# One batch turn of an attention and maxout kernel put in another order: scores inside the first layer, state read beside S.W

## The chip, the cores and the metric

The kernel runs on one core of a Trainium2 chip. A core has a matrix engine (TensorE, PE in the profile, with its weight loads as PEld), three engines for elementwise work (VectorE = DVE, ScalarE = ACT, GpSimd = POOL) and a queue engine (SyncE = SP) that here issues all transfers of the loop. TensorE writes only into eight PSUM banks, and the other engines copy results from there. Engines run side by side, each in its own order, and wait for each other by semaphores. The metric is the device time of one execution, in microseconds.

## The reference, cut to what matters

```python
# x: 8 batches, 8 heads, 512 tokens, 64 wide; state: 8, 8, 32 slots, 64
scale = 1.0 / np.sqrt(D)
scores = scale * np.matmul(x, state.transpose(0, 1, 3, 2))      # 512 x 32
a = softmax(scores)                                             # over the slots
xread = np.matmul(a, state)
scores2 = scale * np.matmul(state, x.transpose(0, 1, 3, 2))     # 32 x 512
sread = np.matmul(softmax(scores2), x)                          # over the tokens
tokens = concatenate([xread, sread], axis=2)    # 8 x 544 tokens of 512 (heads side by side)
return np.maximum(tokens @ w1, tokens @ w2) @ w_out             # w1, w2: 512 x 1024; w_out: 1024 x 512
```

## The kernel before, in words

`max(t w1, t w2) = t w2 + relu(t (w1 - w2))`, so the kernel forms `wd = w1 - w2` and `wwo = w2 w_out` once. The read of a token is linear in the softmax A, so per batch it forms S.W (`sw_mm`: the state's block-diagonal form `sbd` times `wd` and `wwo`) and never writes `xread`. What is done for a batch b:

- x in two casts to bf16: `cast_e` (for the state read, tile `xe`) and `cast_b` (tile `xb`), the latter transposed by a DMA (`xt_dma`, x^T in `xt`);
- `sc_mm`, `sc_ev`: scores from x^T in two halves, 8 matmuls each, exp on ScalarE into `e`; `red` sums and inverts on VectorE, `mul` scales to A (tile `a`) on GpSimd, and `at_dma` transposes A by a DMA into `at`;
- `sr_mm`: the state read, 32 matmuls of `e` with `xe` in TensorE tiles of 128 x 32; `sr_ev` scales it by the sums, `sr_tr` and `sr_cp` transpose it into `sread_t`;
- `sw_mm`: 24 matmuls in tiles of 64 x 32 into six half-used banks, evicted by `sw_ev`;
- the first layer: `l1_mm`, 8 pieces f of two 512-column matmuls, relu by `l1_ev` into `r`;
- the second layer as seven `product`s of 8 matmuls of 256 columns instead of eight (sums of halves of r are formed by `r_sum` on VectorE, partial results parked by `keep` and added by `put`), with four `opened` of 4 matmuls that add A^T times S.W's part for `wwo`;
- `store` writes the 1 MB of results.

The table `ORDER` writes out by hand the order of the weights' work and of batches 0 and 1. The loop at the end of the program runs `b` from 2 to 6, one turn each: first and second layer of batch b, together with scores, A, S.W and state read of batch n = b+1, loads of b+4, casts of b+2 and b+3, and a share of the tokens that come from the state. Batch 7 and those tokens follow behind the loop. The order of the calls is the order on each engine; nothing reschedules it. PSUM banks are dealt out by a ring of five ("r") and three fixed ones (`BX`, `BY`, `BZ`) for the products pX, pY, pZ. All transfers of the loop stand in one SP queue in the order of the calls; an issue waits on SP until its semaphores allow it, and what is behind it waits too.

Of the kernel before, what the change touches and what calls it, by code (L numbers as in the profile page):

```python
# [38 lines left out]
rs.0.0>V rs.0.1>V re.1.3>A p2o.1 ldx.3.0 ldx.3.1 ldx.4.0 ldx.4.1 p1.0@1 k0.0>A p1.1@4 rs.0.2>V wt.2>V v00.0 p6.0  # L39
rs.0.3>V k0.1>A k1.0>A p5.0@7 wt.3>V v00.1 rs.1.0>V k2.0>A sc.2.0@6 exp.2.0>A sc.2.1@0 exp.2.1>A sw.2.0@5,3 red.2.0>V  # L40
mul.2.0>P red.2.1>V swe.2.0.0>A swe.2.0.1>A ce.2.0>A ce.2.1>A ce.2.2>A ce.2.3>A p7.0 o7.0 v11.0 rs.1.1>V mul.2.1>P
p3.0 o3.0 rs.1.2>V atd.2 sw.2.w@6,2 swe.2.w.0>A v01.0 swe.2.w.1>A p4.0 o4.0 rs.1.3>V ce.3.0>P cb.3.0>P cb.3.1>P xtd.3
ce.3.1>P ce.3.2>P ce.3.3>P v10.0>A store.0 dif.1>P sr.2@0 p6.1 k1.1>A sw.2.1@5,3 sre.2>V swe.2.1.0>A swe.2.1.1>V
p5.1@7 k2.1>A p7.1 o7.1 v11.1 p3.1 o3.1 v01.1 srt.2@0 srte.2>A p4.1 o4.1 v10.1>A ldx.5.0 ldx.5.1
"""
# [9 lines left out]
def kernel(  # L55
# [9 lines left out]
    nc = tc.nc  # L65
    B, H, S, D = x.shape
# [38 lines left out]
    def many(n, name, shape, dtype=BF16):  # L105
        return [sbuf.tile([128, *shape], dtype, name=f"{name}{i}") for i in range(n)]
# [127 lines left out]
    def cast_b(b, g, eng):  # L234
        copy(eng, xb_s[b % 2][:, :, 256 * g:256 * g + 256].rearrange("p c (i d) -> p i c d", i=4),
             xf(b)[:, 4 * g:4 * g + 4, :].rearrange("p i (c d) -> p i c d", c=NC))

    def xt_dma(b):
        nc.sync.dma_start_transpose(out=xt_s[b % 2].rearrange("p c k t -> p (c k) t"),
                                    in_=xb_s[b % 2].rearrange("p c m -> p (c m)"))  # L240
# [14 lines left out]
    def sc_mm(b, hh, ring="r"):  # L255
        p = bank(ring)
        pv = p.rearrange("p (c g i n) -> p c i g n", c=NC, g=2, i=2)
        for c in range(NC):
            for kk in range(2):
                k = 2 * hh + kk  # L260
                nc.tensor.matmul(pv[:, c, kk], xt_s[b % 2][:, c, k, :], sbd[:, b, k, :],  # L261
                                 start=(c == 0 and kk == 0), stop=(c == NC - 1 and kk == 1))
        return p
# [110 lines left out]
    def l1_mm(b, f, ring="r"):  # L374
        p = bank(ring)
        for g in range(2):
            nc.tensor.matmul(p, sw_s[b % 3][:, g, f * 128:(f + 1) * 128], at_s[b % 3][:, g].rearrange("p c t -> p (c t)"),  # L377
                             start=(g == 0), stop=(g == 1))
# [46 lines left out]
    def product(pv, lhs, rhs, first=False, cc=(0, 1)):  # L425
        for c in cc:
            for f in range(4):
                nc.tensor.matmul(pv[c], lhs[:, f, 128 * c:128 * c + 128], rhs[:, f, :],  # L428
                                 start=first and f == 0 and (c == 0 or pv.split), stop=False, skip_group_check=True)
# [35 lines left out]
    def so_half(b, k):  # L465
        return sw_s[b % 3][:, :, FF + 256 * k:FF + 256 * k + 256]
# [266 lines left out]
    difference(2, "P")  # L733
    for g in range(2):
        cast_b(4, g, "P")
    for b in range(2, B - 1):
        n = b + 1
        if b + 2 < B and b != 3:
            xt_dma(b + 2)
        if b < 4:  # L740
            nc.vector.reciprocal(rr_all[:, b - 2], srd[:, b - 2, 0:130:129])
        for f in range(NF):
            l1_ev(l1_mm(b, f), b, f)
        pX, pY, pZ = Pair(BX), Pair(BY), Pair(BZ)
        pp = [sc_mm(n, hh) for hh in range(2)]
        for hh in range(2):
            sc_ev(pp[hh], n, hh)
        product(pX, rq(b, 0, 0), wq(0, 0), True)
        keep(0, pX, "A")
        r_sum(b, 0, "V")  # L750
        red(n, 0)
        mul(n, 0, "P")
        r_sum(b, 1, "V")
        product(pZ, rq(b, 0, 1), wq(1, 0), True)
        opened(b, pZ, 0, so_half(b, 0))
        pg = [sw_mm(n, 512 * z, 512 * z + 512, BY if z == 0 else "r") for z in range(3)]
        sw_ev(pg[0], n, 0, 512, 0, "A")
        sw_ev(pg[0], n, 0, 512, 1, "A")
        red(n, 1)
        mul(n, 1, "P")  # L760
        at_dma(n)
        if b == 3:
            xt_dma(b + 2)
        if b == 2:
            store(1)
        if b + 4 < B - 1:
            for g in range(2):
                load_x(b + 4, g)
        elif b + 4 < B:
            load_x(b + 4, 0, n=H)  # L770
        r_sum(b, 2, "V")
        product(pX, st[:, 1], wt[:, 1])
        sw_ev(pg[1], n, 512, 1024, 0, "A")
        keep(1, pX, "A")
        put(b, 0, 0, pZ, 0)
        sw_ev(pg[1], n, 512, 1024, 1, "V")
        sw_ev(pg[2], n, 1024, 1536, 0, "A")
        product(pY, st[:, 0], wt[:, 0], True)
        keep(2, pY, "A")
        r_sum(b, 3, "V")  # L780
        sw_ev(pg[2], n, 1024, 1536, 1, "A")
        if b + 2 < B:
            for k in range(4):
                cast_e(b + 2, k, "P")
        difference(n, "P")
        if b + 3 < B:
            for g in range(2):
                cast_b(b + 3, g, "P")
        if b < 6:
            v_sum(b - 2, "P")  # L790
        product(pX, st[:, 2], wt[:, 2])
        opened(b, pX, 1, so_half(b, 1))
# [114 lines left out]
```

## Time and profile before

| | us |
|---|---|
| median of 3 runs (143.96 to 144.49) | 143.96 |
| span of the profiled execution, first to last instruction | 141.9 |
| TensorE busy | 132.1 |
| VectorE busy | 103.9 |
| ScalarE busy | 88.4 |
| GpSimd busy | 72.6 |

Of the profiled execution the page gives its span and no other time. Busy times overlap: a matmul's record runs on until its results stand in the bank, while the next one has already started. For TensorE the differences of starts are therefore read. A row of the timeline has start, length, engine, line, operation, tiles and count. Lines are those of the kernel before; a helper's line (L404 for every addition, L99 for every ScalarE copy) stands for all of its calls. In the changed kernel a line is inserted at L123, so that L404 there is L405, while L99 stays L99.

### The profile page before, as it was taken

How to read it: one execution, taken by the hardware profiler on the slowest of the kernel's cores; microseconds unless marked ns; L12 is line 12 of the kernel's file. 1: busy time of each engine (PE TensorE's matmuls, PEld its weight loads, DVE VectorE, ACT ScalarE, POOL GpSimd, SP SyncE). 2: the span in 40 equal slices, each digit the busy share in tenths (PEclk: the TensorE clock that was granted, in tenths of full speed). 3: DMA queues.
4: the chain of work that ended last, by engine and by line, in shares of the span. 5: the costliest groups of instructions: out<-in, count | busy, mean ns of one | idle time of the engine just before them, and what ended most of it. 6: DMA issues, size and time to landing. Idle time of an engine off the chain costs nothing.

```text
span 141.9 us, 3651 instructions
## 1 busy us (share of the span) xinstructions
PE 132.1 (93%) x1432; PEld 93.6 (66%) x1442; DVE 103.9 (73%) x193; ACT 88.4 (62%) x172; POOL 72.6 (51%) x99
## 2 busy tenths in 40 slices
PE   6585999999999999999999999999999999999980
PEld 2264735456787776786778577857876786788860
DVE  3488969778999748984898489569948986848320
ACT  4367968886599547665874769087737745753220
POOL 4147326089109993599179809963980544200000
PEclk9999999999999999999999999999999999999998
DMA  4999999954999999999947999669217041502073
GB/s 120 332 372 389 388 381 388 347 100 78 180 316 288 72 273 259 248 255 270 390 167 137 222 385 161 134 222 225 48 34 296 2 79 69 229 0 79 2 257 120
DMA packets 36452, 29.50 MB, mean 208 GB/s; under 512 B 22608, under 2 KB 32336, under 8 KB 35536
## 3 DMA queue, kind: packets, MB, share of 16 engines
q1 hardware_dynamic: 36160, 29.10, 74.9%
q8 instruction: 12, 0.20, 0.6%
q10 hardware_dynamic: 272, 0.13, 0.3%
q14 instruction: 8, 0.07, 0.1%
HBM read 15.20 MB, written 8.91 MB: 170 GB/s over the span
## 4 chain that ended last, share of the span: by engine, by line
PE 85%; DMA 6%; DVE 2%; SPq 2%; ACT 1%; issue 1%; DVEq 0%
PE bank L428 36%; PE bank L377 18%; PE bank L434 10%; DMA big<-in_moe_w_dram 6%; PE bank L354 5%; PE bank L608 5%; PE bank L475 2%; PE bank L517 2%; PE bank L261 2%; PE bank L301 2%; SPq L164 1%; PE bank L515 1%; DVE w2m L101 1%; DVE r L372 1%; PE bank L550 1%
## 5 line engine op out<-in xcount | busy, mean ns | idle before, releaser
L372 DVE TENSOR_SCALAR r<-bank 128x512 bf16<-128x512 f32 x32 | 21.9, 690 | 13.0 <-PE bank L377 11.9
L277 POOL TENSOR_TENSOR a<-e,er 128x512 bf16<-128x512 bf16 x14 | 17.2, 1235 | 27.4 <-ACT big L99 16.3
L99 ACT COPY big<-bank 128x512 f32<-128x512 f32 (+2 forms) x40 | 21.9, 552 | 12.8 <-PE bank L434 5.5
L377 PE MATMUL bank<-at,sw 128*128 128x512 bf16 x120 | 29.1, 379 | 0.6 <-DVE sw L101 0.2
L428 PEld LDWEIGHTS <-big 128*128 128x128 bf16 x256 | 23.9, 98 | 6.1 <-DVE big L404 2.1
L99 ACT CAST sw<-bank 128x512 bf16<-128x512 f32 x36 | 20.1, 609 | 6.0 <-PE bank L354 6.0
L428 PE MATMUL bank<-big,big 128*128 128x256 bf16 x192 | 23.1, 273 | 0.1
L404 DVE TENSOR_TENSOR big<-bank,big 128x512 f32<-128x512 f32 (+1 forms) x25 | 16.5, 663 | 8.3 <-PE bank L434 7.9
L377 PEld LDWEIGHTS <-sw 128*128 128x128 bf16 x128 | 12.2, 97 | 13.5 <-ACT sw L99 0.5
L370 ACT ACTIVATE r<-bank 128x512 bf16<-128x512 f32 x32 | 18.3, 596 | 4.1 <-PE bank L377 3.9
L428 PEld LDWEIGHTS <-r 128*128 128x128 bf16 x192 | 18.2, 98 | 2.7 <-issue 0.5
L103 POOL CAST xe<-big 128x512 bf16<-128x512 f32 x23 | 15.6, 709 | 6.2 <-DMA big<-in_x_dram 6.2
L103 POOL CAST xb<-big 128x1024 bf16<-128x1024 f32 x12 | 13.1, 1111 | 4.7 <-DMA big<-in_x_dram 4.7
L428 PE MATMUL bank<-wo,r 128*128 128x256 bf16 x128 | 15.5, 273 | 0.0
L434 PE MATMUL bank<-sw,at 128*128 128x256 bf16 x96 | 14.4, 273 | 0.0
L99 ACT COPY sread_t<-bank 128x128 bf16<-128x128 bf16 x8 | 3.2, 472 | 17.3 <-PE bank L338 14.0
L434 PEld LDWEIGHTS <-at 128*128 128x128 bf16 x128 | 12.5, 98 | 1.7
L404 DVE TENSOR_TENSOR big<-r 128x1024 bf16<-128x1024 bf16 x16 | 11.6, 723 | 0.6
L273 DVE TENSOR_REDUCE sums<-e 128x16 f32<-128x512 bf16 x16 | 10.8, 674 | 0.0
L269 ACT ACTIVATE e<-bank 128x512 bf16<-128x512 f32 x16 | 8.9, 596 | 1.9 <-PE bank L261 1.4
L404 POOL TENSOR_TENSOR big<-sw 128x512 bf16<-128x512 bf16 x8 | 9.2, 1150 | 1.3 <-issue 1.3
L101 DVE CAST sw<-bank 128x512 bf16<-128x512 f32 x12 | 7.9, 681 | 1.0 <-PE bank L354 1.0
(100 smaller groups left out, 181.8 us busy)
## 6 DMA issues: line engine op xcount, KB each, us to landing
big<-in_x_dram SPq DMA_DIRECT2D x14, 512.0 KB, 7.8
out_dram<-big SPq DMA_DIRECT2D x7, 1024.0 KB, 6.0
big<-in_moe_w_dram SPq DMA_DIRECT2D x8, 512.0 KB, 11.5
big<-in_moe_w_out_dram SPq DMA_DIRECT2D x4, 512.0 KB, 11.0
big<-in_x_dram SPq DMA_DIRECT2D x1, 1024.0 KB, 6.9
out_dram<-big SPq DMA_DIRECT2D x4, 256.0 KB, 2.7
sf<-in_state_dram SPq DMA_DIRECT2D x1, 384.0 KB, 10.4
out_dram<-w2m SPq DMA_DIRECT2D x2, 128.0 KB, 2.4
```

Source lines behind the costliest of these rows:

```text
L99: nc.scalar.copy(o, i)
L101: nc.vector.tensor_copy(o, i)
L103: nc.gpsimd.tensor_copy(o, i)
L269: nc.scalar.activation(out=e_view(e_s[b % 2], hh).rearrange("p (g c) i n -> p g c (i n)", g=2), in_=p.rearrange("p (c g m) -> p g c m", c= ...
L273: nc.vector.tensor_reduce(es_all[:, b, hh], e_view(e_s[b % 2], hh), axis=AXX, op=ALU.add)
L277: (nc.gpsimd if eng == "P" else nc.vector).tensor_mul(e_view(a_s[b % 2], hh), e_view(e_s[b % 2], hh), er_s[b % 2][:, hh].unsqueeze(3).to_b ...
L370: nc.scalar.activation(out=o, in_=p, func=ACTF.Relu)
L372: nc.vector.tensor_scalar(o, p, scalar1=0.0, scalar2=None, op0=ALU.max)
L377: nc.tensor.matmul(p, sw_s[b % 3][:, g, f * 128:(f + 1) * 128], at_s[b % 3][:, g].rearrange("p c t -> p (c t)"), start=(g == 0), stop=(g = ...
L404: (nc.gpsimd if eng == "P" else nc.vector).tensor_tensor(o, i0, i1, op=op)
L428: nc.tensor.matmul(pv[c], lhs[:, f, 128 * c:128 * c + 128], rhs[:, f, :], start=first and f == 0 and (c == 0 or pv.split), stop=False, ski ...
L434: nc.tensor.matmul(pv[c], at_s[b % 3][:, g, 2 * i + c, :], rhs[:, g, :], start=False, stop=False, skip_group_check=True)
```

## The change

The turn is written in another order:

- `sc_mm` of batch b+1 stands inside the first layer (first half behind piece 1, second half behind piece 3), in banks BZ and BY in place of the ring; `red` and `mul` follow behind pieces 1 and 5, and `at_dma` is issued right behind the layer. The layer's eight evictions go to ScalarE and VectorE by the letters AVAVAAAV in place of in turn.
- The state read moves from behind the fifth product to behind the first, right in front of S.W, in bank BZ. ScalarE copies its 130 columns into `raw`, a piece of SBUF; `sr_ev` later reads that.
- The second product and its opening move from in front of S.W to behind it.
- `xt_dma(b+3)` is issued right behind `cast_b(b+3)`, in the turn in which the cast is made, in place of the head of the next turn (in b = 3: behind that turn's `at_dma`). GpSimd does these casts ahead of `difference`.
- In `ORDER`, `cast_b` and the transposition of batch 3 go ahead of its first `cast_e`.
- The flag that chooses the general path (a matmul and a copy) moves from the end of turn 6 to behind the first layer of batch 7.

```diff
-p3.0 o3.0 rs.1.2>V atd.2 sw.2.w@6,2 swe.2.w.0>A v01.0 swe.2.w.1>A p4.0 o4.0 rs.1.3>V ce.3.0>P cb.3.0>P cb.3.1>P xtd.3
+p3.0 o3.0 rs.1.2>V atd.2 sw.2.w@6,2 swe.2.w.0>A v01.0 swe.2.w.1>A p4.0 o4.0 rs.1.3>V cb.3.0>P cb.3.1>P xtd.3 ce.3.0>P
...
+    raw = rs_o[:, 0, 0:130]
...
+    xt_dma(4)
     for b in range(2, B - 1):
         n = b + 1
-        if b + 2 < B and b != 3:
-            xt_dma(b + 2)
...
         for f in range(NF):
-            l1_ev(l1_mm(b, f), b, f)
-        pX, pY, pZ = Pair(BX), Pair(BY), Pair(BZ)
-        pp = [sc_mm(n, hh) for hh in range(2)]
-        for hh in range(2):
-            sc_ev(pp[hh], n, hh)
-        product(pX, rq(b, 0, 0), wq(0, 0), True)
-        keep(0, pX, "A")
-        r_sum(b, 0, "V")
-        red(n, 0)
-        mul(n, 0, "P")
-        r_sum(b, 1, "V")
-        product(pZ, rq(b, 0, 1), wq(1, 0), True)
-        opened(b, pZ, 0, so_half(b, 0))
-        pg = [sw_mm(n, 512 * z, 512 * z + 512, BY if z == 0 else "r") for z in range(3)]
...
-        red(n, 1)
-        mul(n, 1, "P")
+            l1_ev(l1_mm(b, f), b, f, "AVAVAAAV"[f])
+            if f in (1, 3):
+                sc_ev(sc_mm(n, f // 2, (BZ, BY)[f // 2]), n, f // 2)
+            if f in (1, 5):
+                red(n, f // 4)
+                mul(n, f // 4, "P")
         at_dma(n)
-        if b == 3:
-            xt_dma(b + 2)
...
+        pX, pY, pZ = Pair(BX), Pair(BY), Pair(BZ)
+        product(pX, rq(b, 0, 0), wq(0, 0), True)
+        r_sum(b, 0, "V")
+        r_sum(b, 1, "V")
+        keep(0, pX, "A")
+        copy("A", raw, sr_mm(n, BZ)[:, 0:130])
+        pg = [sw_mm(n, 512 * z, 512 * z + 512, BY if z == 0 else "r") for z in range(3)]
+        sw_ev(pg[0], n, 0, 512, 0, "A")
+        sw_ev(pg[0], n, 0, 512, 1, "A")
+        product(pZ, rq(b, 0, 1), wq(1, 0), True)
+        opened(b, pZ, 0, so_half(b, 0))
...
-        difference(n, "P")
         if b + 3 < B:
             for g in range(2):
                 cast_b(b + 3, g, "P")
+            xt_dma(b + 3)
+        difference(n, "P")
...
-        p = sr_mm(n, "r")
-        put(b, 1, 1, pX, 2)
-        sr_ev(p, n)
+        sr_ev(raw, n)
...
+        put(b, 1, 1, pX, 2)
```

On TensorE the state read (L301 before, L302 now) and S.W (L354, L355) come together. Here is the entry into S.W of turn b=2, before, with the opening of the second product (L434) ahead of it:

```order
L434 LDWEIGHTS at2_101
L434 MATMUL bank0_63<-sw2_104,at2_101 128x256
L354 LDWEIGHTS sbd0_74
L354 MATMUL bank7_70<-wd0_75,sbd0_74 32x512
L354 LDWEIGHTS sbd0_74
```

And now, the same place, with the end of the state read ahead of it:

```order
L302 LDWEIGHTS e1_92
L302 MATMUL bank0_63<-xe0_84,e1_92 32x65
L355 LDWEIGHTS sbd0_74
L355 MATMUL bank7_70<-wd0_75,sbd0_74 32x512
L355 LDWEIGHTS sbd0_74
```

S.W used to follow 256-column matmuls on the whole array; it now follows the state read's small tiles.

SP's queue from the x^T of batch 4 (xt0) on, before; `at` rows are A^T, `out` rows are stores, `in_x` rows loads:

```order
L239 DMA_TRANSPOSE xt0_87<-xb0_89 128x16x128
L282 DMA_TRANSPOSE at0_99<-a1_94 128x8x128
L470 DMA out_0_dram<-big2_111 128x2048
L164 DMA big8_117<-in_x_dram 128x4x256 x2
L470 DMA out_0_dram<-big7_116 128x2048
L282 DMA_TRANSPOSE at1_100<-a0_93 128x8x128
L239 DMA_TRANSPOSE xt1_88<-xb1_90 128x16x128
L164 DMA big0_109<-in_x_dram 128x8x256
```

And now:

```order
L240 DMA_TRANSPOSE xt0_87<-xb0_89 128x16x128
L283 DMA_TRANSPOSE at0_99<-a1_94 128x8x128
L471 DMA out_0_dram<-big2_111 128x2048
L165 DMA big8_117<-in_x_dram 128x4x256 x2
L240 DMA_TRANSPOSE xt1_88<-xb1_90 128x16x128
L471 DMA out_0_dram<-big7_116 128x2048
L283 DMA_TRANSPOSE at1_100<-a0_93 128x8x128
L165 DMA big0_109<-in_x_dram 128x8x256
```

The x^T of batch 5 (xt1) moved up past batch 4's A^T (at1) and past store 2 (big7).

On ScalarE, the part of turn b=2 from the last scores' exp or relu to the last S.W cast, before (big6 is where `keep` parks, sw0 is S.W of batch 3):

```order
L269 ACTIVATE e1_92<-bank3_66 128x8x64
L99 COPY big6_115<-bank4_67 128x512
L99 CAST sw0_102<-bank7_70 128x512
L99 CAST sw0_102<-bank1_64 128x512
L99 CAST sw0_102<-bank6_69 128x512
L99 COPY big6_115<-bank4_67 128x512
L99 CAST sw0_102<-bank5_68 128x512
L99 COPY big6_115<-bank7_70 128x512
L99 CAST sw0_102<-bank3_66 128x512
```

And now:

```order
L371 ACTIVATE r0_105<-bank6_69 128x512
L99 COPY big6_115<-bank4_67 128x512
L99 COPY w2m0_80<-bank0_63 128x130
L99 CAST sw0_102<-bank7_70 128x512
L99 CAST sw0_102<-bank5_68 128x512
L99 CAST sw0_102<-bank3_66 128x512
L99 CAST sw0_102<-bank6_69 128x512
L99 COPY big6_115<-bank4_67 128x512
L99 CAST sw0_102<-bank2_65 128x512
```

A copy of 130 columns (w2m, the tile that `raw` is a part of) stands behind the first parked product, and one S.W cast more ahead of the second.

More of the change, by code (lines that the diff above doesn't have):

```diff
@@ L742 @@
         for f in range(NF):
-            l1_ev(l1_mm(b, f), b, f)
-        pX, pY, pZ = Pair(BX), Pair(BY), Pair(BZ)
-        pp = [sc_mm(n, hh) for hh in range(2)]
-        for hh in range(2):
-            sc_ev(pp[hh], n, hh)
-        product(pX, rq(b, 0, 0), wq(0, 0), True)
-        keep(0, pX, "A")
-        r_sum(b, 0, "V")
-        red(n, 0)
-        mul(n, 0, "P")
-        r_sum(b, 1, "V")
-        product(pZ, rq(b, 0, 1), wq(1, 0), True)
-        opened(b, pZ, 0, so_half(b, 0))
-        pg = [sw_mm(n, 512 * z, 512 * z + 512, BY if z == 0 else "r") for z in range(3)]
-        sw_ev(pg[0], n, 0, 512, 0, "A")
-        sw_ev(pg[0], n, 0, 512, 1, "A")
-        red(n, 1)
-        mul(n, 1, "P")
+            l1_ev(l1_mm(b, f), b, f, "AVAVAAAV"[f])
[4 more added lines that the diff above has]
+                mul(n, f // 4, "P")
         at_dma(n)
-        if b == 3:
-            xt_dma(b + 2)
         if b == 2:
@@ L770 @@
             load_x(b + 4, 0, n=H)
+        pX, pY, pZ = Pair(BX), Pair(BY), Pair(BZ)
[9 more added lines that the diff above has]
+        opened(b, pZ, 0, so_half(b, 0))
         r_sum(b, 2, "V")
+        sw_ev(pg[1], n, 512, 1024, 0, "A")
         product(pX, st[:, 1], wt[:, 1])
-        sw_ev(pg[1], n, 512, 1024, 0, "A")
+        sw_ev(pg[1], n, 512, 1024, 1, "V")
+        put(b, 0, 0, pZ, 0)
+        sw_ev(pg[2], n, 1024, 1536, 0, "A")
         keep(1, pX, "A")
-        put(b, 0, 0, pZ, 0)
-        sw_ev(pg[1], n, 512, 1024, 1, "V")
-        sw_ev(pg[2], n, 1024, 1536, 0, "A")
         product(pY, st[:, 0], wt[:, 0], True)
+        sw_ev(pg[2], n, 1024, 1536, 1, "A")
         keep(2, pY, "A")
         r_sum(b, 3, "V")
-        sw_ev(pg[2], n, 1024, 1536, 1, "A")
         if b + 2 < B:
@@ L792 @@
         opened(b, pX, 1, so_half(b, 1))
-        p = sr_mm(n, "r")
-        put(b, 1, 1, pX, 2)
-        sr_ev(p, n)
+        sr_ev(raw, n)
         if b < 4:
             srd_ev(b - 2)
+        put(b, 1, 1, pX, 2)
+        product(pY, st[:, 3], wq(1, 1))
+        opened(b, pY, 0, so_half(b, 1))
         if n == B - 1:
             check_sums()
-        product(pY, st[:, 3], wq(1, 1))
-        opened(b, pY, 0, so_half(b, 1))
         put(b, 0, 1, pY, 1)
@@ L811 @@
                 m_sum(k, aq, sst, "P")
-            p = bank("r")
-            nc.tensor.matmul(p[:, 0:1], full, bad, start=True, stop=True)
-            nc.vector.tensor_copy(flag[0:1, :], p[0:1, 0:1])
         store(b)
@@ L820 @@
         l1_ev(l1_mm(b, f), b, f)
-    for k in (0, 1, 2, 3):
+    p = bank("r")
+    nc.tensor.matmul(p[:, 0:1], full, bad, start=True, stop=True)
+    r_sum(b, 0, "V")
+    nc.vector.tensor_copy(flag[0:1, :], p[0:1, 0:1])
+    for k in (1, 2, 3):
         r_sum(b, k, "V")
```

## The prediction

> **What bounds the kernel now.** I read the head of the page first, then its chain, then busy times turn by turn, then one turn on TensorE in order of time.
>
> ```profile
> span 141.9 us, 3651 instructions
> PE 132.1 (93%) x1432; PEld 93.6 (66%) x1442; DVE 103.9 (73%) x193; ACT 88.4 (62%) x172; POOL 72.6 (51%) x99
> PE 85%; DMA 6%; DVE 2%; SPq 2%; ACT 1%; issue 1%; DVEq 0%
> ...
> 65.33:78.61 13.28, 13.23 (x164) 9.57 (x163) 10.18 (x19) 8.99 (x19) 9.39 (x11) 1.00 0.78 228
> ```
>
> The last row is turn b=3 of the loop (window, its length, then busy time of PE, PEld, DVE, ACT, POOL, the granted clock, the DMA share, GB/s). TensorE is busy 13.23 of 13.28 us at granted clock 1.00, and 85% of the chain is its own. No engine makes it wait by much, so earlier scores, an earlier A and an earlier x^T have no large wait to remove. A gain must come out of TensorE's own row of work, and a loss comes from anything that now arrives late. Here is turn b=3 on TensorE (start, length, line):
>
> ```profile
> 65.33 3.62 PE L377 MATMUL bank<-at,sw 128*128 128x512 bf16 x15
> 68.79 0.63 PE L261 MATMUL bank<-sbd,xt 128*128 128x64 bf16 x16
> 69.25 1.91 PE L428 MATMUL bank<-wo,r 128*128 128x256 bf16 x16
> 71.00 0.60 PE L434 MATMUL bank<-sw,at 128*128 128x256 bf16 x4
> 71.53 0.63 PE L354 MATMUL bank<-wd,sbd 64*32 64x512 bf16 x16
> 71.97 0.40 PE L354 MATMUL bank<-wwo,sbd 64*32 64x512 bf16 x8
> 72.30 2.84 PE L428 MATMUL bank<-big,big 128*128 128x256 bf16 x24
> 74.98 0.60 PE L434 MATMUL bank<-sw,at 128*128 128x256 bf16 x4
> 75.51 0.43 PE L301 MATMUL bank<-xe,e 128*32 128x65 bf16 x32
> 75.87 1.05 PE L428 MATMUL bank<-wo,big 128*128 128x256 bf16 x8
> 76.75 0.60 PE L434 MATMUL bank<-sw,at 128*128 128x256 bf16 x4
> 77.19 1.04 PE L428 MATMUL bank<-big,r 128*128 128x256 bf16 x8
> 78.06 0.60 PE L434 MATMUL bank<-big,at 128*128 128x256 bf16 x4
> 78.61 1.24 PE L377 MATMUL bank<-at,sw 128*128 128x512 bf16 x4
> ```
>
> Differences of starts are the true cost, since the lengths overlap. Four opening matmuls (L434) cost 0.44 (76.75 to 77.19), but 0.53 ahead of S.W (71.00 to 71.53) and 0.53 ahead of the state read (74.98 to 75.51). So going from the whole array into the small tiles 64\*32 or 128\*32 costs 0.09. Leaving costs as much: 16 S.W matmuls take 0.44, 0.22 for eight, and the last eight take 0.33 until the product starts (71.97 to 72.30), 0.11 more. For the state read, whose rows are merged, I take the same 0.11. Two visits to small tiles: 0.40 us of a turn.
>
> One more small wait: the three products from 72.30 take 2.68, against 3 x 0.87 = 2.61 by the product at 77.19. The third must wait until ScalarE has copied the first one's sum (`keep(1)`) out of its bank:
>
> ```profile
> 72.00 1.56 ACT L99 CAST sw<-bank 128x512 bf16<-128x512 f32 x3 [1.04 <-PE bank L354]
> 73.44 0.61 ACT L99 COPY big<-bank 128x512 f32<-128x512 f32 x1
> 73.92 0.62 ACT L99 CAST sw<-bank 128x512 bf16<-128x512 f32 x1
> ```
>
> The copy ends at 74.05 and the third product was due at 72.30 + 1.75 = 74.05; it starts about 0.05 late. The copy was held by three S.W casts ahead of it on ScalarE.
>
> **The change part by part.**
>
> *State read right in front of S.W* (turns b=2 to 6). Before: in, out, in, out, 0.40. After: in (0.09), state read to S.W (x), out (0.11). No row shows a change from 128\*32 to 64\*32 tiles. Lower bound for x: 0, it costs nothing to stay in small tiles. Upper bound: 0.11, the dearest change of tile size. All four changes that the rows show cost 0.09 to 0.11, so I take x = 0.10: 0.10 saved a turn, 0.50 in five; with x = 0 it is 0.20 and 1.0. The Trainium skill, "TensorEngine Tiling (Array Packing)", Key Properties, says that changing the tiling mode drains the engine and moving to another tile of the same mode does not, and it lists 128x32 and 64x32 as different modes. By that rule x is one more drain and the sum below stands; without it the time is that of the first rival. No run here shows this change of mode.
>
> *S.W casts ahead of more work.* A product and its opening (0.87 + 0.44) now stand between S.W and the product that `keep(1)` reads, so ScalarE's casts are done when it ends. That takes away the 0.05: 0.25 in five turns. Lower bound 0.
>
> *Scores inside the first layer.* The same 16 score matmuls, as twice 8. They use the whole array, and the rows show no cost for going there from L377 or from there to a product (68.79 to 69.25 is 0.46, 0.029 each), so I take 0. The evictions crowd, though:
>
> ```profile
> L372 DVE TENSOR_SCALAR r<-bank 128x512 bf16<-128x512 f32 x32 | 21.9, 690 | 13.0 <-PE bank L377 11.9
> L370 ACT ACTIVATE r<-bank 128x512 bf16<-128x512 f32 x32 | 18.3, 596 | 4.1 <-PE bank L377 3.9
> L273 DVE TENSOR_REDUCE sums<-e 128x16 f32<-128x512 bf16 x16 | 10.8, 674 | 0.0
> L274 DVE RECIPROCAL er<-sums 128x16 f32<-128x16 f32 x16 | 4.0, 253 | 1.1
> L99 ACT COPY big<-bank 128x260 f32<-128x260 f32 x4 | 1.5, 377 | 0.5 <-PE bank L323 0.5
> ```
>
> The layer with the scores lasts 3.46 + 0.46 = 3.92 us. VectorE has three relus and two reductions with reciprocals in it, 3 x 0.69 + 2 x 0.93 = 3.93; ScalarE five relus and two exps of about 0.6, 4.2. Both are full, but late evictions have cover. The first product reads pieces f0 to f3; the last of these on VectorE ends at about 1.1 + 0.69 + 0.93 + 0.69 = 3.4 after the layer's start, before 3.92. The second product reads f4 to f7, done at about 5.0, and starts at 3.92 + 0.87 + 0.09 + 0.36 + 0.77 = 6.0, since state read and S.W now stand ahead of it. Cost 0. If that cover were gone, each late microsecond would count five times.
>
> *The copy of the state sums* (`raw`). The second product writes the bank that the state read used, so it waits for this copy on ScalarE. `keep(0)` starts at about 5.0, the next copy 0.48 later (73.44 to 73.92), and this one has 130 columns, at most the 0.377 of 260: done at 5.86, 0.16 before 6.0. I take 0. VectorE's two scalings then read SBUF; they wait for nothing.
>
> *GpSimd.* Two casts of batch b+3 go ahead of `difference`, which ends 2 us later; its reader is the last opening of the next turn, some 10 us off. 0.
>
> *Flag after the last layer.* One matmul and one small copy change place; DVE's copy is needed only after the 3.5 us of state layers. 0.
>
> *x^T behind its cast, A earlier.* This reorders SP's queue, and here lies the risk:
>
> ```profile
> 52.05 3.62 PE L377 MATMUL bank<-at,sw 128*128 128x512 bf16 x15
> ...
> 48.54 1.92 SPq L239 DMA_TRANSPOSE xt<-xb  x1
> ...
> 54.55 6.18 SPq L239 DMA_TRANSPOSE xt<-xb  x1
> 61.01 1.23 SPq L282 DMA_TRANSPOSE at<-a  x1
> 62.34 0.52 SPq L470 DMA_DIRECT2D out_dram<-big  x1
> 62.91 1.69 SPq L164 DMA_DIRECT2D big<-in_x_dram  x2
> 74.39 1.24 SPq L282 DMA_TRANSPOSE at<-a  x1
> ...
> xt<-xb SPq DMA_TRANSPOSE x1, 4.3
> xt<-xb SPq DMA_TRANSPOSE x1, 8.2
> xt<-xb SPq DMA_TRANSPOSE x1, 10.0
> at<-a SPq DMA_TRANSPOSE x1, 3.1
> at<-a SPq DMA_TRANSPOSE x1, 3.2
> out_dram<-big SPq DMA_DIRECT2D x1, 1024.0 KB, 6.0
> out_dram<-big SPq DMA_DIRECT2D x1, 1024.0 KB, 3.8
> ```
>
> The first row is the layer of b=2, the next are SP's issues. The lower rows are times from issue to landing: x^T issued at 48.54, at 54.55 and once later, A^T at 61.01 and 74.39, the store of 62.34 and one of an empty queue. Batch 4's A^T landed at 74.39 + 3.2 = 77.6, 1.0 before its layer at 78.61. In the changed kernel x^T of batch 5 goes ahead of store 2, and both wait on SP ahead of this A^T; what SP waits for there, it all waits for. SP is free for it after the loads, at 62.91 + 1.69 = 64.6; its cast is done by then, because A's multiplications on GpSimd move ahead by 3 us. It stands behind a store and two loads like the one of 54.55, which blocked SP for 6.18 and landed after 8.2: SP free at 70.8, landing 72.8. Store 2 follows; from the last transposition's landing to a store's landing took 68.3 - 64.1 = 4.2 at 62.34, and 3.8 from an empty queue: 76.6 to 77.0. A^T goes behind it; behind x^T it landed 64.1 - 62.75 = 1.35 later: 78.0 to 78.35. Two turns shortened by 0.15 want it at 78.31. So it is just in time; I take 0.1 of waiting. With the transposition that took 10.0 it is 80.2, 1.85 late; the best case is 0. Of the later turns, batch 5's layer is due 13 us later with nothing but x^T and one 1 MB load added ahead of its store; I take 0.
>
> Before the loop, x^T of batch 3 landed at 48.54 + 4.3 = 52.84. Its scores now start at 52.05 + 2 x 0.43 = 52.91 in place of 52.05 + 3.46 = 55.5. It is issued up to 1 us earlier, since one cast moves behind it, so it is in time, by little: 0, at worst some tenths, which the wait at batch 4 would swallow.
>
> Sum: -0.50 - 0.25 + 0.10 = -0.65. The profiled execution shows only its span, 141.9; the runs' median, 143.96, is 2.06 above, for what lies around the span. 141.9 - 0.65 + 2.06 = 143.3.
>
> **The rivals.**
>
> *Staying in small tiles is free (x = 0).* For it: inside S.W eight tiles run side by side with no gap. Against: every change of tile size in the rows costs 0.09 or more. It saves 1.0 + 0.25: 142.7.
>
> *A^T of batch 4 is late (the other side).* Place: start of turn b=4; price: 1 us for each us after 78.31, because TensorE has no slack later to win it back. From 79.1 on it eats the whole saving, from 79.8 on the kernel is slower by over 0.5%. For it: the 10.0 row, which alone gives 80.2 and 143.96 - 0.75 + 1.85 = 145.1. Against: that transposition met the next batch's traffic, this one has the 8.2 row's neighbours. The Trainium skill, "DMA: Bandwidth & Descriptors", Queues, rings and completion order, says that each DMA engine takes a queue's descriptors in ring order. By it A^T can't pass the store, and this rival's sum stands.
>
> *ScalarE holds the second product* by the copy of the state sums: it decides when that copy ends over 0.16 later than worked out. 0.3 a turn would be 1.5 - 0.7, about 144.8. Against: rows with 0.48 spacing.
>
> *Nothing comes of it*: x is 0.11 and `keep(1)` is still late, 0.45 saved and some tenths of waiting: 143.7, no measurable change.
>
> **How the numbers follow.** What a measurement can tell from no change is about 0.5%, 0.72 us: 143.24 to 144.68 is the same. Forecast (x charged, A^T less than 0.3 late) 0.50, at 143.2 to 143.55; x free 0.15; A^T late by 0.3 to 1.5, or nothing of it, 0.20, at 143.5 to 144.7; late by more, or ScalarE holding, 0.15, 144.7 to 145.3. The forecast lies at the border of faster: I give 0.20 of its 0.50 to that side. Faster 0.35, same 0.50, slower 0.15. The range 142.6 to 144.8 leaves out the far end of the last case and a little on the other side.
>
> **What would show it.** On TensorE a turn of about 13.1; from the state read's first start to the second product 0.36 - 0.11 + 0.10 + 0.77 = 1.12 (free: 1.02); no 0.05 ahead of the third product; a gap ahead of L1 at b=4 with A^T named as releaser, or none. Gaps in all five turns ahead of the second product would mean ScalarE, a layer longer than 3.92 the evictions. Either makes the prediction wrong, and so does an x^T of batch 3 that lands long after 52.9.

## The result: 151.0 us, slower by 4.7%

The changed kernel takes 151.04 us (median of 4 runs, 150.69 to 151.32) beside 144.05 us for the kernel before in the same comparison: ratio 1.047, 95% interval 1.045 to 1.050. The forecast was 143.3 us, range 142.6 to 144.8. The profiled execution shows a span of 148.9 us in place of 141.9.

From the page of the changed kernel: its head, busy times, shares of the chain, then two turns by window (columns as in the prediction: window, length, then PE, PEld, DVE, ACT and POOL busy) and TensorE's waits in the loop (for whom, us in total, times, longest):

```profile
span 148.9 us, 3664 instructions
PE 135.5 (91%) x1442; PEld 95.2 (64%) x1442; DVE 113.0 (76%) x188; ACT 90.5 (61%) x182; POOL 75.6 (51%) x99
PE 59%; DVE 21%; DMA 6%; issue 4%; ACT 3%; SPq 2%; POOL 1%; DVEq 0%; ACTq 0%
67.19:82.51 15.32, 13.65 (x166) 9.48 (x163) 12.44 (x18) 9.36 (x21) 10.37 (x10) 1.00 1.16 257
112.14:125.24 13.10, 13.10 (x165) 9.63 (x163) 11.25 (x21) 8.60 (x18) 3.29 (x3) 1.00 0.31 102
PE bank L429 <- DVE big L405: 5.5, 8, 1.2
```

VectorE's share of the chain went from 2% to 21%, and its busy time from 103.9 to 113.0 us with the same additions and scalings to do. By the starts of the first layers (52.40, 67.19, 82.51, 97.77, 112.14, 125.24) the five turns last 14.79, 15.32, 15.26, 14.37 and 13.10 us, against 13.28, 13.28, 13.22, 13.22 and 13.26 before: b=2 to 5 lose 6.7 us and b=6 gains 0.16, which makes 6.6 of the 7.0 us. Of the rest, 0.35 lie ahead of the loop, where kernels that differ only inside it scatter as much (first layer of b=2 at 52.43 in the run with scores and A early, at 52.03 in the one with the state read scaled on ScalarE). In b=6 GpSimd is busy for 3.29 us, in b=3 for 10.37. The waits row says where: in front of products TensorE waits for an addition on VectorE.

Turn b=3 of the changed kernel, the part that answers to the turn shown of before (TensorE, VectorE and GpSimd in order of start):

```profile
72.08 0.43 PE L302 MATMUL bank<-xe,e 128*32 128x65 bf16 x32
72.44 0.62 PE L355 MATMUL bank<-wd,sbd 64*32 64x512 bf16 x16
72.68 1.10 DVE L405 TENSOR_TENSOR big<-r 128x1024 bf16<-128x1024 bf16 x1
73.18 3.67 POOL L103 CAST xe<-big 128x512 bf16<-128x512 f32 x4
73.21 1.05 PE L429 MATMUL bank<-wo,r 128*128 128x256 bf16 x8
73.81 0.98 DVE L405 TENSOR_TENSOR big<-big,r 128x1024 bf16<-128x1024 bf16 x1
74.72 1.09 DVE L405 TENSOR_TENSOR big<-r 128x1024 bf16<-128x1024 bf16 x1
74.85 2.81 PE L429 MATMUL bank<-big,big 128*128 128x256 bf16 x24 [0.16 <-DVE big L405]
76.80 2.48 POOL L103 CAST xb<-big 128x1024 bf16<-128x1024 f32 x2
76.93 1.44 DVE L405 TENSOR_TENSOR big<-r,big 128x1024 bf16<-128x1024 bf16 x1
78.43 1.05 PE L429 MATMUL bank<-wo,big 128*128 128x256 bf16 x8 [0.33 <-DVE big L405]
78.48 1.95 DVE L310 TENSOR_SCALAR sr<-w2m,sums 128x64 bf16<-128x64 f32 x2
79.24 1.15 POOL L405 TENSOR_TENSOR big<-sw 128x512 bf16<-128x512 bf16 x1
79.31 0.60 PE L435 MATMUL bank<-sw,at 128*128 128x256 bf16 x4
80.36 1.28 DVE L405 TENSOR_TENSOR big<-bank,big 128x512 f32<-128x512 f32 x2
81.09 1.03 PE L429 MATMUL bank<-big,r 128*128 128x256 bf16 x8 [1.18 <-DVE big L405]
```

Read it from the bottom. The last product starts at 81.09, though its forerunner (four openings, 0.44 by their starts) began at 79.31: 1.34 late. It needs the bank that `put(1,1)` empties (first of the two at 80.36), and `put(1,1)` stands on VectorE behind the two scalings of 78.48, which take 1.95 us. Nothing here waits by a semaphore: the scalings run, only slowly. The relu sums too (`r_sum`: 72.68, 73.81, 74.72, 76.93) take 0.98 to 1.44 us and hold two products by 0.32 and 0.49.

The same two steps in turn b=3 of the kernel before:

```profile
72.83 0.63 DVE L404 TENSOR_TENSOR big<-r 128x1024 bf16<-128x1024 bf16 x1
73.06 1.30 POOL L277 TENSOR_TENSOR a<-e,er 128x512 bf16<-128x512 bf16 x1 [0.19 <-DVE er L274]
74.31 2.74 POOL L103 CAST xe<-big 128x512 bf16<-128x512 f32 x4
74.57 0.89 DVE L404 TENSOR_TENSOR big<-r,big 128x1024 bf16<-128x1024 bf16 x1
76.58 0.48 DVE L309 TENSOR_SCALAR sr<-bank,sums 128x64 bf16<-128x64 f32 x2
...
114.30 0.68 DVE L404 TENSOR_TENSOR big<-r,big 128x1024 bf16<-128x1024 bf16 x1
```

There the scalings take 0.48 for two beside GpSimd's casts, reading the bank; the one relu sum that meets a cast takes 0.89, and the same sum of turn b=6 (last row), where no cast runs, 0.68. The sum of 72.83 starts ahead of a multiplication of A and keeps its 0.63; the multiplication takes 1.30, in the changed kernel 1.05. Grouped by form (count, busy us, mean ns), first of before, then of after:

```profile
L309 DVE TENSOR_SCALAR sr<-bank,sums 128x64 bf16<-128x64 f32 x12 | 2.9, 280 | 0.2
L404 DVE TENSOR_TENSOR big<-r 128x1024 bf16<-128x1024 bf16 x16 | 11.6, 723 | 0.6
L103 POOL CAST xe<-big 128x512 bf16<-128x512 f32 x23 | 15.6, 709 | 6.2 <-DMA big<-in_x_dram 6.2
```

```profile
L310 DVE TENSOR_SCALAR sr<-w2m,sums 128x64 bf16<-128x64 f32 x10 | 9.2, 965 | 0.2
L310 DVE TENSOR_SCALAR sr<-bank,sums 128x64 bf16<-128x64 f32 x2 | 0.5, 280 | 0.0
L405 DVE TENSOR_TENSOR big<-r 128x1024 bf16<-128x1024 bf16 x16 | 15.5, 971 | 0.6
L103 POOL CAST xe<-big 128x512 bf16<-128x512 f32 x23 | 19.3, 871 | 6.4 <-DMA big<-in_x_dram 6.4
```

The ten scalings that now read SBUF (tile `w2m`, where `raw` lies) take 965 ns, the two that still read a bank 280. Sums and casts are slower on both sides. By the starts of single matmuls, TensorE waits in front of the last product for 1.34, 1.34, 1.34 and 1.19 us (5.2 in all, the scalings) and for relu sums 0.29, 0.32 + 0.49, 0.32 + 0.49 and 0.09 (2.0). That is more than the 5.5 of the waits row, since that row counts from the end of a matmul's record, 0.16 after the next one could have started. 7.2 of loss less the 0.65 forecast as a saving is 6.55; the turns show 6.6.

The theory: VectorE and GpSimd hold each other up where both work on SBUF, and the change brings two kinds of VectorE work into that: the scalings by reading SBUF, the relu sums because A's multiplications, and with them the casts, run 3 us earlier on GpSimd. The rivals: only the casts do it; the moved state read does it by its copy or place, whatever reads it; A's earlier place does all of it. The experiments stand in that order. Each is compared with the kernel before on the same chip.

### The profile page after: what moved, and what is told of

It is laid out like the page before. It is cut to its first block, busy times and chain, and to the rows that moved or that the text cites. A ratio compares the mean times of both kernels' runs of the same rounds, so it can differ in the third digit from the quotient of the medians.

```text
span 148.9 us, 3664 instructions
## 1 busy us (share of the span) xinstructions
PE 135.5 (91%) x1442; PEld 95.2 (64%) x1442; DVE 113.0 (76%) x188; ACT 90.5 (61%) x182; POOL 75.6 (51%) x99
## 4 chain that ended last, share of the span: by engine, by line
PE 59%; DVE 21%; DMA 6%; issue 4%; ACT 3%; SPq 2%; POOL 1%; DVEq 0%; ACTq 0%
PE bank L429 21%; PE bank L378 14%; DVE big L405 11%; DMA big<-in_moe_w_dram 6%; PE bank L435 6%; PE bank L609 4%; DVE sr L310 4%; PE bank L355 3%; PE bank L476 2%; DVE sw L101 2%; PE bank L518 2%; PE bank L262 2%; DVE r L373 1%; POOL a L278 1%; SPq L165 1%
## 5 line engine op out<-in xcount | busy, mean ns | idle before, releaser
L378 PE MATMUL bank<-at,sw 128*128 128x512 bf16 x128 | 31.1, 379 | 0.2 <-DVE sw L101 0.2
L278 POOL TENSOR_TENSOR a<-e,er 128x512 bf16<-128x512 bf16 x14 | 14.7, 1051 | 28.2 <-ACT e L270 19.2
L373 DVE TENSOR_SCALAR r<-bank 128x512 bf16<-128x512 f32 x27 | 17.8, 666 | 12.4 <-PE bank L378 12.1
L103 POOL CAST xe<-big 128x512 bf16<-128x512 f32 x23 | 19.3, 871 | 6.4 <-DMA big<-in_x_dram 6.4
L371 ACT ACTIVATE r<-bank 128x512 bf16<-128x512 f32 x37 | 20.7, 610 | 2.2 <-PE bank L378 2.2
L99 ACT CAST sw<-bank 128x512 bf16<-128x512 f32 x36 | 19.2, 600 | 0.9 <-PE bank L355 0.9
L103 POOL CAST xb<-big 128x1024 bf16<-128x1024 f32 x12 | 14.5, 1228 | 4.7 <-DMA big<-in_x_dram 4.7
L429 PE MATMUL bank<-wo,r 128*128 128x256 bf16 x128 | 16.3, 273 | 0.0
L405 DVE TENSOR_TENSOR big<-r 128x1024 bf16<-128x1024 bf16 x16 | 15.5, 971 | 0.6
L429 PE MATMUL bank<-big,r 128*128 128x256 bf16 x64 | 8.3, 272 | 4.6 <-DVE big L405 4.6
```

The costliest lines, as they stand in the source:

```text
L99: nc.scalar.copy(o, i)
L103: nc.gpsimd.tensor_copy(o, i)
L278: (nc.gpsimd if eng == "P" else nc.vector).tensor_mul(e_view(a_s[b % 2], hh), e_view(e_s[b % 2], hh), er_s[b % 2][:, hh].unsqueeze(3).to_b ...
L371: nc.scalar.activation(out=o, in_=p, func=ACTF.Relu)
L373: nc.vector.tensor_scalar(o, p, scalar1=0.0, scalar2=None, op0=ALU.max)
L405: (nc.gpsimd if eng == "P" else nc.vector).tensor_tensor(o, i0, i1, op=op)
```

## The experiments

**Without the casts.** The changed kernel less its casts in the loop.

```diff
-            for k in range(4):
-                cast_e(b + 2, k, "P")
...
-            for g in range(2):
-                cast_b(b + 3, g, "P")
```

> The changed kernel without GpSimd's casts of x in the loop (cast_e and cast_b left out, the state read and x^T then use old data). Theory 1 (VectorE's operations from SBUF to SBUF wait for GpSimd's casts): the two scalings of the state sums fall from 0.98 us each to about 0.25, r_sum from up to 1.44 to 0.7, all waits of TensorE for VectorE in the turns go, turns of 13.1 and 143.2 to 143.8 us in all. Theory 2 (the scaling is slow because it reads SBUF, and stands ahead of put(1,1)): it stays near 0.98, TensorE still waits some 1.2 us a turn, 148 to 150 us. Theory 3 (A^T or the evictions come late): no change in the waits, about 150.

Measured: 145.53 us, ratio 1.008 (1.006 to 1.010). Most of the loss is gone, and the relu sums are at 0.68 to 0.69 but for the first of a turn, which meets a multiplication of A (1.09) and holds nothing up. But the time is above the expectation: in two turns the last product still waits, 0.92 and 0.86. (In the change it is 1.34, since there the slow relu sums also bring VectorE late to the scalings: 1.27 us ahead of the time at which the last product of b=3 was due, here 1.94.) The scalings of b=2 and of b=3 in this kernel, with what GpSimd does beside them:

```profile
61.91 0.42 DVE L310 TENSOR_SCALAR sr<-w2m,sums 128x64 bf16<-128x64 f32 x2
...
75.47 1.15 POOL L405 TENSOR_TENSOR big<-sw 128x512 bf16<-128x512 bf16 x1 [3.67 <-DMA out_dram<-big]
75.58 2.20 DVE L310 TENSOR_SCALAR sr<-w2m,sums 128x64 bf16<-128x64 f32 x2
76.58 1.15 POOL L405 TENSOR_TENSOR sb<-wwo,sb 128x512 bf16<-128x512 bf16 x1
```

In b=2 GpSimd is idle until 62.29 and two scalings from SBUF take 0.42. In b=3, with the casts gone, `difference` and `v_sum` run where the scalings are, and the two take 2.20: one ends at 76.67, the other at 77.78, and the two additions on GpSimd at 76.62 and 77.73. So each scaling lasts until the GpSimd instruction beside it ends. The theory had to be widened from "casts" to "GpSimd's work on SBUF".

**The scalings behind the addition.** In the changed kernel `sr_ev(raw, n)` goes behind `put(b, 1, 1, pX, 2)`; nothing gets faster, only its place is another.

> The changed kernel with sr_ev behind put(1,1) as before, GpSimd's casts as in the change. Theory 1: the scalings and r_sum stay slow, but nothing waits for the scalings: of the 7.2 us of waits the 5.2 ahead of the last product go, the 2.0 for r_sum stay, about 145.8 us. Theory 2: the whole loss was the scaling's place, 143.5 to 144. Theory 3: 150 to 151.

Measured: 145.77 us, 1.012 (1.010 to 1.014), as the theory had it: the waits of 1.2 to 1.3 are gone from all four turns, those for relu sums (0.30; 0.09 + 0.50; 0.32 + 0.50; 0.09) remain. In b=2 the state transposes then wait 0.49 for the scaling.

**The casts moved off the relu sums.** The four `cast_e` stand at the head of the turn, beside the layer; `difference` and `v_sum` come ahead of `cast_b`.

```diff
+            for k in range(4):
+                cast_e(b + 2, k, "P")
         for f in range(NF):
             l1_ev(l1_mm(b, f), b, f, "AVAVAAAV"[f])
```

> The changed kernel with GpSimd's order alone changed: cast_e at the head of the turn, beside the first layer, where VectorE reads PSUM; cast_b and x^T behind difference and v_sum. sr_ev stays ahead of put(1,1). Theory 1: r_sum about 0.7, the scalings 0.25 to 0.6 (difference can still meet them), 143.3 to 144.5 us. Theory 2: the scaling keeps 0.98 and its place, 147 to 149. Theory 3: 150 or more, since x^T is later.

Measured: 146.58 us, 1.017 (1.015 to 1.018): too high for the expectation. The relu sums are down to about 0.69, but `difference` and `v_sum` now run beside the scalings, 2.20 for two in three turns, and the last product waits 0.86 to 0.92 there. In b=2 a relu sum that meets a multiplication of A costs 0.38.

**The same, and the scalings on ScalarE.** VectorE keeps the reciprocal.

```diff
-        sr_ev(raw, n)
+        nc.vector.reciprocal(rr_all[:, n], raw[:, 0:130:129])
+        for g in range(2):
+            nc.scalar.activation(out=sr_s[n % 2][:, g, :], in_=raw[:, 1 + 64 * g:65 + 64 * g], func=ACTF.Copy,
+                                 scale=rr_all[:, n, g:g + 1])
```

> As e4_casts_in_layer, and the state sums are scaled on ScalarE from the copy in SBUF, so that VectorE has only the reciprocal ahead of put(1,1). Theory 1: no wait of TensorE for VectorE in the turns is left, turns of 13.1, 143.2 to 143.6 us, 0.3 to 0.6% under the kernel before. Theory 2: the same within 0.5 us. Theory 3: 150 or more.

Measured: 143.87 us, 0.999 (0.997 to 1.000), a little above the expected 143.2 to 143.6. One wait of 0.40 is left, in b=2, where a relu sum (1.42 us) meets a multiplication of A.

**The scalings on ScalarE alone.** That edit in the changed kernel, with the casts where the change has them.

> The changed kernel with one edit: the state sums are scaled on ScalarE, VectorE has only their reciprocal. Casts stay where the change has them. My theory: the 1.2 to 1.3 us ahead of the last product go in each of the four turns; the relu sums still meet the casts and keep their 1.8 us, and 0.65 is saved on TensorE: 144.05 + 1.8 - 0.65 = 145.2 us (144.8 to 145.8). Rival (the waits of the relu sums and those of the scalings are one, whichever VectorE work is in front): 148 or more.

Measured: 145.51 us, 1.009 (1.006 to 1.012), as expected. This one edit gives back 5.5 of the 7 us; its turn b=3, where VectorE goes straight from the reciprocal to `put(1,1)`:

```profile
76.80 2.48 POOL L103 CAST xb<-big 128x1024 bf16<-128x1024 f32 x2
...
77.22 0.67 DVE L405 TENSOR_TENSOR big<-bank,big 128x512 f32<-128x512 f32 x1
77.39 0.59 ACT L793 ACTIVATE sr<-w2m,sums 128x64 bf16<-128x64 f32 x2 [1.04 <-DVE sums L791]
78.60 1.04 PE L429 MATMUL bank<-big,r 128*128 128x256 bf16 x8
```

The product at 78.60 waits for nothing; ScalarE scales both from SBUF in 0.59 while GpSimd runs. The relu sums are as slow as in the changed kernel (992 ns on the mean).

**The parts of the change, each alone in the kernel before.** First the state read in front of S.W, copied to `raw` and scaled from there behind `put(1,1)` (the change itself has the scalings ahead of it).

```diff
+        copy("A", raw, sr_mm(n, "r")[:, 0:130])
         pg = [sw_mm(n, 512 * z, 512 * z + 512, BY if z == 0 else "r") for z in range(3)]
...
-        p = sr_mm(n, "r")
         put(b, 1, 1, pX, 2)
-        sr_ev(p, n)
+        sr_ev(raw, n)
```

> The kernel before with one part of the change: the state read stands right in front of S.W, ScalarE copies its sums to SBUF, VectorE scales them from there behind put(1,1), as in the change. A and the scores stay where they were. My theory (the loss is VectorE's SBUF work meeting GpSimd's SBUF work, and A's earlier place is what brings both the relu sums and the scalings onto GpSimd's busy stretches; TensorE's saving of mode changes is real): the relu sums no longer meet GpSimd, so turns of 13.13 to 13.2 and a saving of up to 0.65, 143.4 us; the scalings still read SBUF and go from 0.24 to about 1 us each where a GpSimd cast, difference or v_sum runs beside them, so a turn may lose up to 1.3 in front of its last product as in the change: 143.4 if they fall into a stretch of GpSimd's silence, up to 146 if not. Rival (the moved state read itself costs, by the copy on ScalarE or the order of the products): 145 or more with waits ahead of the second product or S.W.

Measured: 145.80 us, 1.011 (1.006 to 1.016). The relu sums have their old means (724, 816, 747 ns); the scalings take 805 ns on the mean, and TensorE waits for them elsewhere than in the change:

```profile
77.34 2.22 DVE L310 TENSOR_SCALAR sr<-w2m,sums 128x64 bf16<-128x64 f32 x2
77.39 1.15 POOL L405 TENSOR_TENSOR big<-sw 128x512 bf16<-128x512 bf16 x1
78.48 2.02 POOL L103 CAST xb<-big 128x1024 bf16<-128x1024 f32 x2
...
79.62 0.23 PE L339 MATMUL bank<-ident,sr 128*128 128x128 bf16 x1 [0.60 <-DVE sr L310]
```

The transpose of the scaled state (L339) is 0.77 late by its start, in b=4 by 0.82. Behind b=2 the first layer waits 0.35 for a late A^T; the next expectation counts this among the waits at the state transposes, where it doesn't belong. The order on VectorE and GpSimd's work are those of before; what differs is where the scaling reads and where the state read stands, and the next run parts the two.

Next, the same with the two scalings on ScalarE.

> The kernel before with the state read in front of S.W, its sums copied to SBUF by ScalarE and scaled there by ScalarE; VectorE has the reciprocal alone. It is the run of the state read moved alone (145.8 us) with the two scalings on another engine. My theory: ScalarE keeps its pace beside GpSimd, so the waits of 0.35 to 0.82 us at the state transposes go, turns of 13.10 to 13.16, 143.4 us (143.1 to 143.8). Rival (those waits come from the copy or the place, not from VectorE beside GpSimd): 145 or more again.

Measured: 144.00 us beside 144.39, 0.998 (0.996 to 1.001). The waits for the scaling are gone: 1.3% less than the run above by the two ratios, from the engine alone, so the state read's place and its copy aren't what cost. Turns b=3 to 6 last 13.14 to 13.20; b=2 lasts 13.61, because A^T of batch 3 landed 4.6 us after its issue (3.1 in the kernel before), 0.43 after TensorE wanted it. The median lies above the expected 143.1 to 143.8 (runs of 143.24 to 144.84).

Then the state read scaled straight out of its bank, ahead of S.W's tiles.

```diff
+        red(n, 1)
+        mul(n, 1, "P")
+        sr_ev(sr_mm(n, "r"), n)
         pg = [sw_mm(n, 512 * z, 512 * z + 512, BY if z == 0 else "r") for z in range(3)]
```

> The kernel before with the state read in front of S.W and nothing copied: VectorE scales the sums straight out of the state read's bank, before S.W's tiles go there, with A's second reduction ahead of it. A, the scores, the casts and x^T stay where they were. My theory (what the state read's move costs alone is VectorE scaling from SBUF beside GpSimd's SBUF work): a scaling that reads PSUM stays at 0.28 us, nothing waits for it, and TensorE's saving of one visit to small tiles less one change between them is left, 0.13 us a turn: turns of 13.10 to 13.16, 143.4 us (143.1 to 143.8). Rival (the moved state read itself costs, through the second relu pair or the banks): 144.2 or more, with waits at the products. Rival (the saving was never there): 144.05, turns of 13.25.

Measured: 149.11 us, 1.035 (1.032 to 1.039): the scaling's price was right, the rest wrong.

```profile
73.37 0.38 PE L354 MATMUL bank<-wwo,sbd 64*32 64x512 bf16 x1
...
73.71 0.25 DVE L274 RECIPROCAL er<-sums 128x16 f32<-128x16 f32 x1
73.88 0.11 DVE L307 RECIPROCAL sums<-bank 128x2 f32<-128x2 f32 x1
74.02 0.48 DVE L309 TENSOR_SCALAR sr<-bank,sums 128x64 bf16<-128x64 f32 x2
...
74.55 0.41 PE L354 MATMUL bank<-wwo,sbd 64*32 64x512 bf16 x7 [0.80 <-DVE sr L309]
```

Two scalings from the bank take 0.48, as before. But S.W wants that bank at once, and the scaling stands behind A's second reduction, so S.W stops for about 1 us in each turn: by the starts, 1.17 from 73.37 to 74.55, and 1.03 to 1.17 in the others. The copy to `raw` has a purpose: it frees the bank early. (In a first form of this kernel the scaling stood behind S.W's tiles, which had written over the bank by then; the flag chose the general path, 550.35 us, and it tells nothing on this question.)

The other large part: scores in the layer and A from there, and all else as before.

> The kernel before with the other part: next batch's scores inside the first layer and A made there, all else as before (state read behind the second-last opening, scaled from the bank, x^T as before). My theory: A's multiplications on GpSimd come 3 us earlier, so its casts start 3 us earlier and meet the relu sums on VectorE, which cost 0.3 + 0.8 + 0.8 + 0.1 of waiting over the loop as in the changed kernel; the scalings read PSUM and stay at 0.28: 144.05 + 1.8 = 145.9 us (145.2 to 146.4). Rival (the whole loss comes from scores and A early): 151. Rival (nothing of the loss lies in A's place, all of it in the scalings): 144.0.

Measured: 146.08 us, 1.012 (1.008 to 1.017). The size is as expected, its make-up not quite. The scalings read their bank and stay at 280 ns, and `big<-r` is at 966 ns; but TensorE waits for two things (b=3):

```profile
71.29 0.72 PE L428 MATMUL bank<-wo,r 128*128 128x256 bf16 x5 [0.16 <-DVE r L372]
...
73.50 1.26 PE L428 MATMUL bank<-big,big 128*128 128x256 bf16 x10 [0.28 <-DVE big L404]
```

By the starts, relu sums cost 0.16, 0.35, 0.35, 0.35 and 0.06 us in the five turns, 1.3 in all. The other 0.85 is the second product, which here comes right behind the first and waits for the layer's last relu (0.33, 0.33, 0.09, 0.10 from b=3 on), late behind the two reductions. The changed kernel has state read and S.W in between and doesn't wait there.

And x^T behind its cast, alone.

> The kernel before with the third part alone: x^T of a batch issued right behind its cast, the cast ahead of the difference. My theory: nothing waits for x^T or for the difference, before or after, so no change: 144.0 us (143.8 to 144.4), turns of 13.2 to 13.3. Rival (x^T ahead of the store and of A's transpose makes A late): 145 or more, with a wait of TensorE for A ahead of the layer of batch 4.

Measured: 144.30 us beside 144.39, 1.000 (0.996 to 1.004). Nothing changes on the median. In the profiled execution (144.78) A^T of batch 4 is late once:

```profile
74.70 1.48 SPq L282 DMA_TRANSPOSE at<-a  x1
...
79.38 0.81 PE L377 MATMUL bank<-at,sw 128*128 128x512 bf16 x3 [0.30 <-DMA at<-a]
```

It landed at 79.34, 4.64 us after its issue, in place of 3.25 before. In the new order it stands behind store 2, which landed at 78.42, 0.92 ahead of it; TensorE waited for 0.47. That is the rival in small, and the risk that the prediction worked out for this queue. The median shows no such cost, and no other execution of this kernel was traced.

**A version that keeps the saving.** The changed kernel with the scalings on ScalarE, and GpSimd's turn in the order `difference`, `v_sum`, the two `cast_b`, the four `cast_e`. The latter run into the next layer, where VectorE reads mostly banks.

```diff
         difference(n, "P")
         if b < 6:
             v_sum(b - 2, "P")
         if b + 3 < B:
             for g in range(2):
                 cast_b(b + 3, g, "P")
             xt_dma(b + 3)
+        if b + 2 < B:
+            for k in range(4):
+                cast_e(b + 2, k, "P")
```

> The changed kernel with the state sums scaled on ScalarE, and GpSimd's order in a turn changed to difference, v_sum, the two casts for x^T, then the four casts for the next state read, which thus run into the next turn's first layer. It differs from the run with casts in the layer (143.87 us) in that the four casts no longer stand ahead of A's multiplications in the turn of batch 2. My theory: the one wait left in that run, 0.40 us in the turn of batch 2 where a relu sum met a multiplication of A, goes too, so every turn is 13.08 to 13.2 and the time is 143.4 us (143.1 to 143.8), relu sums near 0.7 us. Rival (the four casts now hold A's multiplications, or the loads on SP, in the later turns): waits for a relu sum or for A^T in several turns, 144.2 or more.

Measured: 143.37 us (143.25 to 143.75, 10 runs) beside 144.06: ratio 0.994, interval 0.992 to 0.996, as expected: 0.6% below the kernel before, which is little but clear of the noise. The first relu sum of each turn still meets a multiplication of A (1.09 us), and nothing waits for it. Its head, and the first and last of its turns:

```profile
span 141.4 us, 3644 instructions
PE 131.7 (93%) x1432; PEld 94.1 (67%) x1442; DVE 99.5 (70%) x178; ACT 93.1 (66%) x192; POOL 68.6 (48%) x99
52.14:65.29 13.15, 13.10 (x163) 9.65 (x162) 9.28 (x17) 9.53 (x21) 7.99 (x9) 1.00 1.11 273
...
104.65:117.72 13.07, 13.02 (x162) 9.60 (x162) 10.17 (x19) 9.13 (x20) 4.29 (x5) 1.00 0.31 102
```

GpSimd is busy for 68.6 us in place of 75.6 with the same instructions: what VectorE no longer loses, GpSimd doesn't either. The five turns sum to 65.58 us, against 66.26 before: 0.68 saved.

## Why the prediction was wrong

Step by step:

- *The scalings: the step that failed.* "VectorE's two scalings then read SBUF; they wait for nothing." I priced the copy, its bank and its semaphores, and took the scaling's own length as unchanged; nor did I price their new place, ahead of `put(1,1)` in place of behind it. It was 280 ns from the bank and 965 from SBUF, up to 1.2 us where a whole GpSimd instruction ran beside it. With `put(1,1)` behind it, that is 1.34, 1.34, 1.34 and 1.19 us: 5.2 us in place of 0. Taking it off VectorE gave 5.5 us back, putting it behind `put(1,1)` 5.3.
- *GpSimd at 0: wrong as well.* I asked only who reads GpSimd's results and when, not what runs beside it. I had seen that A's multiplications "move ahead by 3 us", but not that the casts follow them onto the relu sums: 2.0 us, and as much lies between the run with only the scalings on ScalarE and the last version, which differ in GpSimd's order alone (145.51 and 143.37). The profile before held the clue, the relu sum of 0.89 beside a cast against 0.68 for the same sum in b=6.
- *TensorE's modes: right.* In the changed kernel the state read starts at 72.08, S.W at 72.44 and the second product at 73.21: 1.13, against the 1.12 of the forecast with x = 0.10 and 1.02 with x = 0. By the forecast's own sum that makes x 0.11 for going from 128\*32 to 64\*32 tiles, so the rival of a free change falls. The drain between modes in the Trainium skill, "TensorEngine Tiling (Array Packing)", Key Properties, agrees.
- *`keep(1)`: nearly right.* The wait ahead of the third product went from 0.05 to 0.02. Turn b=6, without GpSimd's casts, lasts 13.10, the forecast's 13.1, and the last version's 0.68 is the forecast's 0.75 before its 0.10 for A^T, within a tenth.
- *Evictions and the copy on ScalarE: right.* The layer with the scores lasts 3.92 (67.19 to 71.11), as worked out. No wait ahead of the second product in the change, where state read and S.W cover the late relus; the run with scores and A early shows 0.85 us of waiting once that cover is gone, as the forecast feared. The rival of ScalarE falls.
- *A^T and x^T: in time, and the queue's chain right.* x^T of batch 5 landed at 72.70 (forecast 72.8), store 2 at 77.03 (76.6 to 77.0), A^T of batch 4 at 77.94 (78.0 to 78.35) and x^T of batch 3 at 52.11; no first layer of the changed kernel waited for a transfer. The turns were so long by then that this kernel doesn't test how tight it was. The last version, with short turns, has A^T at 77.41, 1.05 ahead of its layer; the run with x^T alone has it 0.47 late.

That the two engines hold each other up is shown in four ways: the same scaling at 0.21 us from SBUF with GpSimd idle, about 1.1 beside `difference` or `v_sum`, 0.24 from a bank beside casts, and unharmed on ScalarE. The traces also show the order: the one that starts second waits for the other's end. All 35 scalings from SBUF of over 0.3 us, in five runs, end 0.05 us behind the GpSimd instruction beside them (three of them started 0.04 ahead of it, which isn't enough; those that started 0.07 or more ahead took 0.25). In the turns b=2 to 6 of all traces but the 550 us one, the 112 relu sums that start while a GpSimd instruction has over 0.1 us to run end 0.54 to 0.55 behind it, and where a multiplication of A starts during a sum, it ends 0.90 to 0.91 behind the sum. So the kernel before had the same meetings, but there GpSimd mostly started second and paid, and nothing waited for it; with A made earlier VectorE more often starts second. Through what they meet, no run shows. The Trainium skill, "SBUF — State Buffer", Who interferes with whom, says that VectorE and GpSimd share one pair of ports as an exclusive lock; that VectorE takes it with two SBUF inputs (against GpSimd work that reads SBUF), or in its two-port modes, which a scaling from SBUF to SBUF may enter; and that the other one blocks until the end of the instruction. The rows agree: scalings end 0.05 us behind the GpSimd instruction beside them, sums with two SBUF inputs go from 0.68 to 1.1, and a scaling from a bank is untouched, as "VectorE: DVE Perf Modes", Why PSUM operands drop a tier, has it (an operand in a bank keeps an instruction out of those modes).

What stays open: whether the scaling from SBUF would be harmless in a form that doesn't enter such a mode (it wasn't tried), and why A^T of batch 3 landed 1.4 to 1.5 us later in the two runs with the state read moved (4.5 and 4.6 from its issue in place of 3.1), behind the same transfers as before.

## What to carry to other kernels

When an operand moves from PSUM to SBUF, or GpSimd's work moves in time, lay VectorE's and GpSimd's rows side by side for the whole stretch and price each overlap of SBUF work on both, even though no semaphore joins them. A short VectorE instruction can cost as much as the GpSimd instruction beside it, and everything queued behind it pays. Which of the two pays is decided by which starts second, so a move in time alone can shift the cost onto the engine that TensorE waits for. The same instruction with two lengths in one profile is the sign that such a meeting exists.

## What was not expected of the hardware

- A 128x64 scaling takes 0.21 us from SBUF alone, 0.24 from a bank beside GpSimd, and about 1.1 from SBUF beside 1.15 us additions of GpSimd.
- Either side can lose, whichever starts second: a multiplication of A takes 1.30 where it starts during a relu sum (the sum 0.63) and 1.05 where it starts first (the sum 1.09 to 1.10). GpSimd's 128x512 casts take 709 ns on the mean before, 871 in the change and 643 in the last version.
- A transposing DMA of A landed 3.0 us after its issue at best. Queued behind a store (batch 4's, in the eight runs with x^T moved up) it took 4.6 to 6.9 us and landed 0.8 to 0.9 behind that store.
